# Two kv heads in one 4 MB unit: larger transfers and fewer slots in a decode attention kernel

## The chip, the cores and the metric

The kernel runs on one core of one Trainium2 chip. The core has a matrix engine (PE, whose weight loads the profile lists apart as PEld), a vector engine (DVE), a scalar engine (ACT), a general engine (POOL) and a queue engine (SP). In this kernel SP issues every transfer between HBM and the on-chip memory (SBUF, 128 partitions); sixteen DMA engines carry them out. Matrix products land in PSUM, eight banks of 512 fp32 numbers for each partition.

The metric is device time in microseconds for one launch. Before the change it is 667.16 us, the median of three runs (666.79 to 667.6). The profiled execution that all rows below come from has a span of 665.6 us, measured from its first instruction to its last.

## What is computed

One decoding step for four sequences (B = 4, one token each, D = 512) through attention, a gated feed-forward block (FFN), and the same two again with the same caches and weights:

```python
        rep = Hq // Hkv
        q = (lambda x, *d: x.transpose(*d))((x @ wq).reshape(B, Sq, Hq, Dh), 0, 2, 1, 3)
        k = jnp.repeat(k_cache, rep, axis=1)
        v = jnp.repeat(v_cache, rep, axis=1)
        scores = jnp.einsum("bhqd,bhkd->bhqk", q, k) * (Dh ** -0.5)
        p = _softmax(scores, axis=-1)
        o = jnp.einsum("bhqk,bhkd->bhqd", p, v)
        return (lambda x, *d: x.transpose(*d))(o, 0, 2, 1, 3).reshape(B, Sq, Hq * Dh) @ wo
...
    def _B_ref(x, w_gate, w_up, w_down):
        g = _silu(x @ w_gate)
        u = x @ w_up
        return (g * u) @ w_down
...
    x = A_x
    x = x + _A_ref(_layernorm(x, axis=-1), A_k_cache, A_v_cache, A_wq, A_wo)
    x = x + _B_ref(_layernorm(x, axis=-1), B_w_gate, B_w_up, B_w_down)
    x = x + _A_ref(_layernorm(x, axis=-1), A_k_cache, A_v_cache, A_wq, A_wo)
    x = x + _B_ref(_layernorm(x, axis=-1), B_w_gate, B_w_up, B_w_down)
    return x
```

All inputs are bf16; Hq = 32, Hkv = 8, Sk = 8192, Dh = 128, F = 1792, so four query heads share a kv head. The two caches hold 4 x 8 x 8192 x 128 numbers each, 67 MB. Each layer reads both. What SBUF can keep from the first layer for the second spares 12 MB of the second reading.

## The kernel before

A unit is one kv head of one sequence: its 8192 keys are 2 MB, its values another 2 MB. There are 32 units for each layer (`NU`). A unit lies in SBUF as 128 partitions of 64 tokens, 16 KB for each partition, so one transfer is 128 rows of 16 KB. SBUF holds eight such slots (`NSLOT`, L139). Six (`NKEEP`) end the first layer with keys and values of the last three units, and the second layer begins with these; the other two take the FFN weights `wg`, `wd` and a part of `wu` at the end of each layer. The other three quarters of `wu` stay in SBUF once loaded.

For each unit, in eight blocks q of eight tokens for each partition:

- `turn` (L393): DVE transposes a block of keys in place, in 32x32 squares of fp32 words (128x512).
- `scores` (L413): four matmuls, each with a 128x128 stationary made of the query (`zq`, written by POOL in `place_q`, L404) and 256 moving key columns. All eight blocks add up in one PSUM bank, whose 128 rows are block, square and query head.
- The softmax of the unit, in steps that `line` spreads over the following blocks: `max_p` on DVE (L419), `max_t` on PE and DVE (L423, L426), `exps` on PE and ACT (L435 to L441), `turn_p` (L444), which transposes the probabilities into `pT`, and `total` (L447, L449) for the sums.
- `values` (L494): 64 matmuls, each with 128x128 values as the stationary and 32 moving columns of `pT`; then `scale_o` (L502).

After four units of a head, `out_proj` (L521) multiplies with `wo` and adds to `x`. `center`, `deviation`, `qproj` and `ffn` do the rest between the layers. `qproj` ends with products on 32-row strips of the output (L573) that place the query for the scores.

The order on PE is written by the program: `blocks` holds what PE is to do next, with a cost for each, and `drain` lets PE lag about 2 us behind the transposes that DVE was given; `advance` lets the steps in `line` in after so much PE work. The keys of a unit come first, then the values of the unit before. All engines run their instructions in order. SP too issues in the order of `items`: `pump` stops at the first one that finds no free slot. At the end of a layer, loads are kept out of slots 6 and 7 (`late`), so that the FFN weights follow the last values directly. The last values of each layer come in four parts (`split`); after the first layer's gate product the place of the weights, and later that of the first kept keys, is refilled in parts (`load_part`).

Resources are tracked by name in `_Sync`: an instruction waits for what last wrote what it reads, and for what last read or wrote what it writes. The first transfer, `A_x` into `scr` (L626), waits for nothing.

Of the kernel before, what the change touches and what calls it, by code (L numbers as in the profile page):

```python
# [5 lines left out]
ACTF = mybir.ActivationFunctionType  # L6
# [97 lines left out]
def bass_interleave_layers__gqa_block_cached__swiglu_ffn__decode_kernel(  # L104
# [17 lines left out]
    REP = Hq // G  # L122
    P = 128
    assert Dh == P and B * Hq == P and D % P == 0 and F % P == 0 and B == 4
# [3 lines left out]
    TT = S // P  # L128
    TB = 8
    NB = TT // TB  # L130
    QB = 32
    NA = P // QB
    assert NB * REP == QB and 2 * 2 * QB == Dh
    SW = TB * QB
    XQ = B * Hq
    assert XQ <= SW
    ZP = QB - REP
    NQ = 4
    NSLOT = 8  # L139
    NKEEP = 6  # L140
    WIDE = 32
    NU = B * G
# [3 lines left out]
    with ExitStack() as es:  # L146
        sb = lambda name, shape, dt: es.enter_context(nc.sbuf_tensor(name, shape, dt))


        SL = TT * Dh  # L150
        FR = KT - 1
        kvf = sb("kvf", [P, NSLOT * SL + FR * F], BF16)
        kv = kvf[:, 0:NSLOT * SL].rearrange("p (s w) -> p s w", s=NSLOT)
        f0 = NKEEP * SL
        wg_sb = kvf[:, f0:f0 + KT * F].rearrange("p (k f) -> p k f", k=KT)
        wu_sb = [kvf[:, NSLOT * SL + k * F:NSLOT * SL + (k + 1) * F] for k in range(FR)]
        wu_sb.append(kvf[:, f0 + KT * F:f0 + (KT + 1) * F])
        f1 = f0 + (KT + 1) * F
        assert f1 + FO * D <= NSLOT * SL
        wd_sb = kvf[:, f1:f1 + FO * D].rearrange("p (f n) -> p f n", f=FO)  # L160
        places = [f"s{s}.{q}" for s in range(NKEEP, NSLOT) for q in range(NB)]
        room = lambda a, b: places[(a - f0) // (TB * Dh):(b - 1 - f0) // (TB * Dh) + 1]
        at_w = {"wg": room(f0, f0 + KT * F) + ["wg"], "wu": room(f0 + KT * F, f1) + ["wu", "wu3"],
                "wd": room(f1, f1 + FO * D)}
        WD = ((0, 6), (6, 12), (12, 14))
        wq_sb = sb("wq_sb", [P, KT, HqDh], BF16)
        wo_sb = sb("wo_sb", [P, Hq, D], BF16)
        identf = sb("identf", [P, P], FP32)

        ident = identf[:].bitcast(BF16).rearrange("p (x e) -> p x e", e=2)[:, :, 1]  # L170
        onesf = sb("onesf", [P, 1], FP32)
        quad = sb("quad", [P, NA], BF16)
        head = sb("head", [P, REP], FP32)
        xT = sb("xT", [P, XB], FP32)
        xs = sb("xs", [P, B], FP32)
        vs = sb("vs", [P, B], FP32)
        xx = sb("xx", [P, XB], FP32)
        lnv = sb("lnv", [P, B], FP32)
        rstd = sb("rstd", [P, B], FP32)
        eps_sb = sb("eps_sb", [P, 1], FP32)  # L180
        lsc_sb = sb("lsc_sb", [P, 1], FP32)
        zero_sb = sb("zero_sb", [P, 1], FP32)
        xc = sb("xc", [P, XB], FP32)
        xn = sb("xn", [P, XB], BF16)
        oT = sb("oT", [P, Hq, B], BF16)
# [507 lines left out]
```

## Time and profile before

| | us |
|---|---|
| median of 3 runs | 667.16 (666.79 to 667.6) |
| span of the profiled execution | 665.6 |
| PE busy, matmuls | 495.1 |
| DVE busy | 380.8 |
| ACT busy | 89.9 |
| DVE transposes of keys, L393, 488 of them | 313.1 |
| PE scores, L413, 2048 of them | 330.0 |
| PE values, L494, 4096 of them | 123.9 |
| DVE idle ahead of L393, waiting for keys | 197.1 |

Transfers move 273.89 MB; the mean over the span is 413 GB/s. A row of the group lists reads: line, engine, operation, output <- inputs, shapes, count, then busy time in us, the mean duration of one in ns, and the idle time of the engine just before them with what ended it. Matmuls overlap in the PE pipeline, so the busy time of one is longer than the distance from one start to the next; the distance is what a row of matmuls costs.

### The profile page before, as it was taken

How to read it: one execution, taken by the hardware profiler on the slowest of the kernel's cores; microseconds unless marked ns; L12 is line 12 of the kernel's file. 1: busy time of each engine (PE TensorE's matmuls, PEld its weight loads, DVE VectorE, ACT ScalarE, POOL GpSimd, SP SyncE). 2: the span in 40 equal slices, each digit the busy share in tenths (PEclk: the TensorE clock that was granted, in tenths of full speed). 3: DMA queues.
4: the chain of work that ended last, by engine and by line, in shares of the span. 5: the costliest groups of instructions: out<-in, count | busy, mean ns of one | idle time of the engine just before them, and what ended most of it. 6: DMA issues, size and time to landing. Idle time of an engine off the chain costs nothing.

```text
span 665.6 us, 16777 instructions
## 1 busy us (share of the span) xinstructions
PE 495.1 (74%) x7400; PEld 393.8 (59%) x7400; DVE 380.8 (57%) x879; ACT 89.9 (14%) x331; POOL 19.9 (3%) x75
## 2 busy tenths in 40 slices
PE   1766676876877777777875999886777787687786
PEld 1554555654755555556665878764665565465565
DVE  1645465664765665665641279775566565476572
ACT  1010111111101101101110112110111111110120
POOL 0000000000000000000000000000000000000000
PEclk9987787777788777878685979977878777778895
DMA  8999999999999999999999999999999999999995
GB/s 357 417 412 405 419 427 426 424 426 427 427 427 422 428 429 425 426 424 427 426 404 367 332 408 425 432 423 424 428 427 426 426 425 426 427 428 425 423 417 226
DMA packets 27320, 274.96 MB, mean 413 GB/s; under 512 B 2408, under 2 KB 6512, under 8 KB 11120
## 3 DMA queue, kind: packets, MB, share of 16 engines
q1 hardware_dynamic: 27248, 273.89, 98.4%
q8 instruction: 58, 0.95, 0.6%
q14 instruction: 14, 0.11, 0.0%
HBM read 273.88 MB, written 0.00 MB: 411 GB/s over the span
## 4 chain that ended last, share of the span: by engine, by line
DMA 68%; PE 16%; SPq 10%; DVE 3%; issue 2%; POOL 0%; ACT 0%; DVEq 0%; POOLq 0%
DMA kvf<-in_A_k_cache_dram 63%; PE ps L413 10%; SPq L93 10%; DMA kvf<-in_B_w_down_dram 5%; PE ps L494 3%; DVE kvf L393 2%; PE ps L435 1%; PE ps L423 1%; DVE pT L444 0%; PE ps L559 0%; DVE mx L419 0%; PE ps L447 0%; PE ps L610 0%; DVE rl L449 0%; PE ps L573 0%
## 5 line engine op out<-in xcount | busy, mean ns | idle before, releaser
L393 DVE STREAM_TRANSPOSE kvf<-kvf 128x512 f32<-128x512 f32 x488 | 313.1, 677 | 197.1 <-DMA kvf<-in_A_k_cache_dram 197.1
L413 PE MATMUL ps<-kvf,zq 128*128 128x256 bf16 x2048 | 330.0, 317 | 9.5 <-DVE kvf L393 5.9
L413 PEld LDWEIGHTS ps<-kvf,zq 128*128 128x128 bf16 x2048 | 212.5, 112 | 71.0 <-DVE kvf L393 11.3
L494 PE MATMUL ps<-pT,kvf 128*128 128x32 bf16 x4096 | 123.9, 179 | 34.9 <-DVE rl L449 32.6
L494 PEld LDWEIGHTS ps<-pT,kvf 128*128 128x128 bf16 x4096 | 120.5, 97 | 42.8 <-issue 37.4
L423 PE MATMUL ps<-identf,mx 128*1 128x128 f32 x64 | 19.8, 309 | 95.7 <-DVE mx L419 95.7
L429 ACT ACTIVATE pb<-m 1x128 f32<-1x128 f32 x64 | 19.7, 308 | 401.6 <-DVE m L426 401.6
L423 PEld LDWEIGHTS ps<-identf,mx 128*1 128x1 f32 x64 | 5.2, 81 | 99.9 <-DVE mx L419 99.8
L404 POOL TENSOR_TENSOR zq<-scr,quad 128x64 bf16<-128x64 bf16 x64 | 18.8, 294 | 617.2 <-PE ps L413 549.2
L435 PEld LDWEIGHTS ps<-onesf,pb 1*128 1x128 f32 x128 | 24.1, 234 | 20.5 <-issue 17.4
L444 DVE STREAM_TRANSPOSE pT<-pb 128x256 bf16<-128x256 bf16 x64 | 26.9, 420 | 13.4 <-ACT pb L439 13.1
L419 DVE TENSOR_REDUCE mx<-ps 128x1 f32<-128x256 f32 x64 | 25.1, 393 | 9.8 <-PE ps L413 9.8
L439 ACT ACTIVATE pb<-ps,nm 128x256 bf16<-128x256 f32 x64 | 30.4, 475 | 2.1
L435 PE MATMUL ps<-onesf,pb 1*128 1x1 f32 x128 | 29.6, 298 | 0.6 <-ACT pb L429 0.5
L438 ACT ACTIVATE nm<-ps 128x1 f32<-128x1 f32 x64 | 11.0, 171 | 132.7 <-PE ps L435 132.7
L447 PEld LDWEIGHTS ps<-rsm,onesf 128*128 128x128 f32 x128 | 20.4, 200 | 2.6 <-ACT rsm L441 0.6
L447 PE MATMUL ps<-rsm,onesf 128*128 128x4 f32 x128 | 19.7, 224 | 0.5 <-ACT rsm L441 0.5
L426 DVE TENSOR_REDUCE m<-ps 1x4 f32<-1x128 f32 x64 | 15.9, 249 | 7.0 <-PE ps L423 6.6
L441 ACT ACTIVATE rsm<-head,rs 128x4 f32<-128x4 f32 x64 | 19.0, 297 | 2.1
L502 DVE TENSOR_TENSOR oT<-ps,rl 128x4 bf16<-128x4 f32 x64 | 7.9, 123 | 10.4 <-PE ps L494 10.1
L559 PE MATMUL ps<-xn,wq_sb 128*128 128x4 bf16 x256 | 7.7, 165 | 8.2 <-DMA wq_sb<-in_A_wq_dram 8.2
L521 PEld LDWEIGHTS ps<-oT,wo_sb 128*128 128x128 bf16 x256 | 8.9, 105 | 6.4 <-DVE oT L502 3.9
(55 smaller groups left out, 91.4 us busy)
## 6 DMA issues: line engine op xcount, KB each, us to landing
kvf<-in_A_k_cache_dram SPq DMA_DIRECT2D x59, 2048.0 KB, 31.3
kvf<-in_A_v_cache_dram SPq DMA_DIRECT2D x58, 2048.0 KB, 32.3
wq_sb<-in_A_wq_dram SPq DMA_DIRECT2D x4, 1024.0 KB, 8.1
wo_sb<-in_A_wo_dram SPq DMA_DIRECT2D x4, 1024.0 KB, 19.2
kvf<-in_A_v_cache_dram SPq DMA_DIRECT2D x8, 512.0 KB, 18.7
kvf<-in_B_w_gate_dram SPq DMA_DIRECT2D x2, 1792.0 KB, 23.3
kvf<-in_B_w_down_dram SPq DMA_DIRECT2D x4, 768.0 KB, 16.4
kvf<-in_A_v_cache_dram SPq DMA_DIRECT2D x2, 1024.0 KB, 6.8
```

Source lines behind the costliest of these rows:

```text
L93: ins = self.eng[engname].dma_start(out_ap, in_ap)
L393: T.op("dve", lambda e: e.transpose(w, w), reads=[f"s{s}.{q}"], writes=[f"s{s}.{q}"])
L413: T.op("pe", lambda e: e.matmul(bank(bk)[:, 0:SW], lhsT=zq[:, c, z0:z0 + P], rhs=w[:, :, c // 2, :, c % 2], start=(q == 0 and c == 0), sto ...
L419: T.op("dve", lambda e: e.tensor_reduce(mx[:], bank(bk)[:, 0:SW], AX.X, ALU.max), reads=[f"pb{bk}"], writes=["mx"])
L423: T.op("pe", lambda e: e.matmul(bank(STEP)[0:1, 0:P], lhsT=mx[:], rhs=identf[:], is_transpose=True, start=True, stop=True), reads=["mx", " ...
L429: T.op("act", lambda e: e.activation(mrow.rearrange("p (x h) -> p x h", h=REP), m4[:].unsqueeze(1).to_broadcast([1, QB, REP]), ACTF.Copy), ...
L435: T.op("pe", lambda e: e.matmul(bank(STEP)[:, 0:1], lhsT=mrow, rhs=onesf[0:1, :], start=True, stop=True), reads=["pb", "onesf"], writes=[f ...
L439: T.op("act", lambda e: e.activation(pb[:], bank(bk)[:, 0:SW], ACTF.Exp, bias=nm[:], accum_out=rs[:]), reads=[f"pb{bk}", "nm"], writes=["p ...
L441: T.op("act", lambda e: e.activation(rsm[:], head[:], ACTF.Copy, scale=rs[:]), reads=["head", "rs"], writes=["rsm"])
L444: T.op("dve", lambda e: e.transpose(pT[:, turn_of[u], 0:SW], pb[:]), reads=["pb"], writes=[f"pT{turn_of[u]}"])
L447: T.op("pe", lambda e: e.matmul(bank(TOT)[:, 0:REP], lhsT=ones, rhs=rsm[:], start=True, stop=True), reads=["rsm", "onesf"], writes=[f"pb{T ...
L494: T.op("pe", lambda e: e.matmul(bank(bk)[:, 0:WIDE], lhsT=kv[:, s, t * Dh:(t + 1) * Dh], rhs=pT[:, turn_of[u], c0:c0 + WIDE], start=(t == ...
```

## The change

A unit becomes a pair of neighbouring kv heads of one sequence. Its keys are 4 MB, as 128 rows of 32 KB (64 partitions for each head), and so are its values; there are 16 pairs (`NP`) for each layer and four slots of 32 KB. Three slots end the first layer with the keys of the last pair and the values of the last two. The order of all loads, with slots and parts, is now a list written ahead (`cmds`); `freed` returns single blocks of a slot, and `pump` issues the next entry when all its blocks are free.

- `turn` takes 128x1024 words, eight of them for a pair (248 in all, from 488). `scores` takes 512 columns instead of 256 (1024 matmuls, from 2048).
- `values` is turned round: the stationary is 32 columns of probabilities, of which `turn_p` fills the half that belongs to the partition's head, the rest being zero, and 512 columns of values stream past it. The outputs of four successive matmuls go to four 32-row strips of one bank. 32 matmuls for a pair, 1024 in all, from 4096. `gather` (four DVE operations on 128x128 words) and `combine` (one matmul and one DVE operation) then pick out and add up what belongs together; nothing of that was there before.
- `exps` loses two ACT operations; the broadcast of the maximum is one small matmul and one DVE operation that multiplies and sums (L464 after). `total` now stands ahead of `turn_p`. `pT`, `rl` and `oT` lose their second copies or shrink. `exps` of a pair now follows the values of the pair before (`behind`), since there is one `pT`.
- In the first layer `qproj` handles all 32 heads at once, ahead of the first keys; in the second eight, then 24 (4 and 28 before). It copies its result by four DVE operations where one did it.
- The FFN weights share one slot with keys and values: slot 0 in the first layer, slot 1 in the second. Slightly less of `wu` stays in SBUF (64 KB more to load in the second layer).
- Small tiles move into `pb`: `A_x` is now loaded into `pb` too, where DVE at the start writes and reads intermediate tables.

The core of the diff:

```diff
-    TB = 8
-    NB = TT // TB
...
+    NP = G // 2 * B
+    TT = 2 * S // P
+    NB = 8
+    TB = TT // NB
...
-    NSLOT = 8
-    NKEEP = 6
...
+    NSLOT = 4
...
+        T.op("dve", lambda e: e.tensor_reduce(pbf[:, 0:QB],
+                                              identf[:].rearrange("p (j x) -> p x j", j=NA), AX.X, ALU.max),
+             reads=["ident"], writes=["pb"])
+        T.op("dve", lambda e: e.tensor_reduce(sel[:].rearrange("p (h r) -> p h r", h=2),
+                                              pbf[:, 0:QB].rearrange("p (h q r) -> p h r q", h=2, q=QH), AX.X, ALU.max),
+             reads=["pb"], writes=["sel"])
+        T.op("dve", lambda e: e.tensor_reduce(own[:], pbf[:, 0:QB].rearrange("p (h q r) -> p q h r", h=2, q=QH),
+                                              AX.XY, ALU.max),
+             reads=["pb"], writes=["own"])
...
+        order = [list(range(NP)), [NP - 1, NP - 2] + list(range(NP - 2))]
...
+        cmds += [(("W", 0), W_SLOT[0], 0, NB)]
+
+        us = order[1]
+        cmds += [(K(1, us[1]), 0, 0, 3), (K(1, us[1]), 0, 3, 4), (K(1, us[1]), 0, 4, NB)]
+        cmds += [(K(1, us[2]), 1, q, q + 2) for q in range(0, NB, 2)]
+        rest = []
+        for i in range(3, NP):
+            rest += [K(1, us[i]), V(1, us[i - 1])]
+        rest.append(V(1, us[-1]))
+        ring = (0, 3, 1, 2)
+        for i, it in enumerate(rest):
+            s = ring[i % NSLOT]
+            if i == 0:
+                cmds += [(it, s, q, q + 2) for q in range(0, NB, 2)]
+            elif i == 1 or i == len(rest) - 1:
+                cmds += [(it, s, q, q + NB // 2) for q in range(0, NB, NB // 2)]
+            else:
+                cmds.append((it, s, 0, NB))
+        cmds += [(("W", 1), W_SLOT[1], 0, NB)]
...
+                    need = {(s, q) for q in range(a, b)}
+                    if not need <= free:
+                        return
+                    free.difference_update(need)
+                    if it[0] == "W":
+                        load_weight("W", it[1], s)
+                    else:
+                        slot_of[it] = s
+                        load(it, a, b, sem_s[s] if b - a == NB else part_sem())
...
+        def freed(s, a, b):
+            free.update((s, q) for q in range(a, b))
+            pump()
...
-            T.op("dve", lambda e: e.transpose(pT[:, turn_of[u], 0:SW], pb[:]), reads=["pb"], writes=[f"pT{turn_of[u]}"])
+            for h in range(2):
+                hp = slice(h * (P // 2), (h + 1) * (P // 2))
+                dst = pT[hp].rearrange("p t n (h x) -> p t n h x", h=2)[:, :, :, h, :]
+                T.op("dve", lambda e: e.transpose(dst, pb[hp]), reads=["pb"], writes=["pT"])
...
+                    step = lambda gap, fn: [gap, u, lambda: fn(u)]
+                    line.extend([step(0.0, max_p), step(1.2, max_t)])
+                    behind.extend([step(0.9, exps), step(1.0, total), step(0.3, turn_p)])
+                    if alone:
+                        line.extend(behind)
+                        behind.clear()
...
-                    T.op("pe", lambda e: e.matmul(bank(bk)[:, 0:WIDE], lhsT=kv[:, s, t * Dh:(t + 1) * Dh],
-                                                  rhs=pT[:, turn_of[u], c0:c0 + WIDE], start=(t == 0), stop=(t == TT - 1)),
-                         reads=[f"s{s}.{q}", f"pT{turn_of[u]}"], writes=[f"pb{bk}"], sig=(t % TB == TB - 1))
...
+                for t in range(t0, t0 + TB // 2):
+                    j = t % NA
+                    first, stop = (h == 0 and t < NA), (h == NH - 1 and t >= TB - NA)
+                    T.op("pe", lambda e: e.matmul(bank(OBK)[j * QB:(j + 1) * QB, :], lhsT=pT[:, t, h, :], rhs=v[:, :, t, :],
+                                                  start=first, stop=stop),
+                         reads=[f"s{s}.{q}" for q in range(h * QH, (h + 1) * QH)] + ["pT"], writes=[f"pb{OBK}"],
+                         sig=(t % (TB // 2) == TB // 2 - 1))
+                if i % 2:
+                    finished(V(L, u), h * QH, (h + 1) * QH)
+                if i == 3:
+                    done.add((L, u))
+                    line[0:0] = rest_
+                    line.extend(behind)
+                    behind.clear()
...
+            def gather():
+                o = lambda q: bank(OBK)[:, q * Dh:(q + 1) * Dh]
+                T.op("dve", lambda e: e.tensor_scalar(acc, o(0), own[:, 0:1], None, op0=ALU.mult),
+                     reads=[f"pb{OBK}", "own"], writes=PB)
+                for q in range(1, QH):
+                    T.op("dve", lambda e: e.scalar_tensor_tensor(acc, o(q), own[:, q:q + 1], acc, op0=ALU.mult, op1=ALU.add),
+                         reads=[f"pb{OBK}", "own", "pb"], writes=["pb"])
+
+            def combine():
+                T.op("pe", lambda e: e.matmul(bank(CMB)[:, 0:H2], lhsT=acc, rhs=sel[:], start=True, stop=True),
+                     reads=["pb", "sel"], writes=[f"pb{CMB}"])
+                T.op("dve", lambda e: e.tensor_tensor(oT[:, gp % 2, :, b], bank(CMB)[:, 0:H2], rl[:], ALU.mult),
+                     reads=[f"pb{CMB}", "rl"], writes=[f"oT{gp % 2}"])
+
+            rest_ = [[0.0, None, gather], [1.3, None, combine]]
+            blocks.extend((0.9, lambda i=i: part(i)) for i in range(4))
...
-        T.dma("sp", xio, A_x.rearrange("b s d -> (b s) d"), sem_x, writes=SCR)
+        T.dma("sp", xio, A_x.rearrange("b s d -> (b s) d"), sem_x, writes=PB)
```

## The prediction

> **What bounds the kernel now.** I read the forty slices first, then the chain of waits, then windows, and then the timeline at the start, between the layers and at the end.
>
> ```profile
> DMA  8999999999999999999999999999999999999995
> GB/s 357 417 412 405 419 427 426 424 426 427 427 427 422 428 429 425 426 424 427 426 404 367 332 408 425 432 423 424 428 427 426 426 425 426 427 428 425 423 417 226
> ...
> q8 instruction: 58, 0.95, 0.6%
> ...
> DMA 68%; PE 16%; SPq 10%; DVE 3%; issue 2%; POOL 0%; ACT 0%; DVEq 0%; POOLq 0%
> ```
>
> The DMA engines are full nearly throughout, at 426 GB/s; 68% of the chain is DMA. A slice is 16.64 us. Against 426 the slices lose about 5 us at the start, 7 to 8 in slices 20 to 23 (the FFN between the layers) and 8 at the end. So what counts is the rate in the steady part, and how long the queue is dry at three places.
>
> ```profile
> 336.00:340.00 4.00, 4.00 (x89) 3.72 (x90) 2.56 (x7) 1.03 (x4) 0.00 (x0) 1.00 0.99 402
> 345.00:349.00 4.00, 1.43 (x28) 1.15 (x24) 1.12 (x7) 0.00 (x0) 0.00 (x0) 0.50 1.04 405
> 100.00:320.00 220.00, 165.44 (x2317) 129.05 (x2314) 132.79 (x295) 28.85 (x108) 6.46 (x22) 0.81 1.01 426
> ```
>
> Windows: the last three columns are granted clock, DMA share and GB/s. Rows of 3.5 and 4 KB move at 402 to 405, rows of 16 KB at 426.
>
> **The change, part by part.**
>
> *Steady part, on the path.* One packet on one of 16 engines takes 142 ns for 3584 bytes (405/16 = 25.3 GB/s) and 615 ns for 16384 (426/16). The line through both has 9 ns for each packet. Rows of 32 KB save half of the packets: 9/1231 = 0.7% of the 600 us that 255.9 MB of keys and values take, 4.4 us. No row of 32 KB is in the trace, so the ends are -4.4 and, if such rows are cut in two, 0; a loss (+3, half a per cent) I can't exclude. I take -3, nearer to the line. Instructions are fetched by the same engines (q8, 0.95 MB); matmuls go from 7264 to 3088, so some 0.5 MB less, -1.3 at 426 GB/s. Sum -4.3, ends -5.7 and +1.7.
>
> *Engines in the steady part, hidden behind DMA.* A pair of units arrives every 19.7 us (8.4 MB at 426).
>
> ```profile
> 28.01 0.40 PE L573 MATMUL ps<-pT,identf 128*32 128x112 bf16 x16 [0.37 <-DVE pT L564]
> ...
> 363.57 5.80 PE L413 MATMUL ps<-kvf,zq 128*128 128x256 bf16 x32 [0.78 <-POOL zq L404]
> ...
> 372.16 1.50 PE L413 MATMUL ps<-kvf,zq 128*128 128x256 bf16 x12
> ...
> 634.60 2.46 DVE L393 STREAM_TRANSPOSE kvf<-kvf 128x512 f32<-128x512 f32 x4
> ```
>
> Scores: 12 in 1.50 us, less the 0.27 that the last takes, is 0.11 us each at full clock; half that speed at half clock. 512 columns take 0.22 or 0.43, so a block of four 0.9 or 1.7, a pair 7 or 13.7 (7 or 13.7 for two units before). Values: the row L573 shows 16 matmuls of 112 columns on four 32-row strips, 0.40 us less a duration of 0.21, 12.7 ns each, where 112 columns alone need 48. Four strips run at once. So 32 matmuls of 512 columns are 8 rounds, 1.7 or 3.4 us (before 2 x 64 x 28 ns = 3.6, hidden too). DVE for a pair: eight transposes of 1024 at 1.2 (two of 0.615), 9.6; maximum over 512, 0.66 (256 took 0.39); minimum row 0.25; `gather`, four at 0.31 (between 56 and 256 words from PSUM, 0.22 and 0.39), 1.25; L464 0.35; `turn_p` 1.4 (256 columns took 0.42, so 0.84 to 1.7 for two of 512); rest 0.3. Sum 13.8 of 19.7, with waits for PE 15. A slot is free about 15 us before its next load is due (keys scored at 14.4, the load that takes their place begins at 29.5). So the new DVE work, ACT's loss of two operations and POOL's 32 instead of 64 `place_q` lie behind DMA; what it costs without that cover is rival 3. The 64 KB more of `wu` are 0.15 us, in the rounding.
>
> *Start.* `A_x` is the first in SP's queue, and `wq` and all caches stand behind it.
>
> ```profile
> 0.75 0.36 SPq L93 DMA_DIRECT2D scr<-in_A_x_dram  x1
> ...
> 1.27 0.09 DVE L247 MEMSET pT<- 128x32 uint32 x1
> ...
> 1.51 0.38 DVE L248 TENSOR_REDUCE head<-identf 128x4 f32<-128x128 f32 x1 [0.15 <-POOL quad L239]
> ...
> 2.17 0.18 PEld L632 LDWEIGHTS ps<-identf,scr 4*128 4x128 bf16 x4 [2.17 <-DMA scr<-in_A_x_dram]
> ```
>
> Now it goes to `pb`, and so waits for the three new reductions there. On DVE: `pT`'s memset starts at 1.27 and takes 0.5 for 512 words (312 took 0.32), `head` 0.4, the next 0.4, `sel` and `own` 0.2 each, with gaps 3.1. SP issues at 3.15 instead of 0.75: +2.4 for everything behind in SP's queue, and DMA has no slack to take it back (ends 2.0 and 2.8).
>
> *End.* In the list of loads the last values go to slot 1 and so do the weights of the second layer, which wait until PE has used all of these values. Nothing but the output stands behind them in SP's queue, but the whole last FFN waits for them. Before, the weights (4.13 MB) followed the values without a gap.
>
> ```profile
> kvf<-in_A_v_cache_dram SPq DMA_DIRECT2D x1, 512.0 KB, 21.3
> ...
> 661.63 1.01 PE L610 MATMUL ps<-scr,kvf 128*128 128x4 bf16 x32 [0.60 <-DMA kvf<-in_B_w_down_dram]
> ```
>
> The last part of the values, issued at 630.4, lands 21.3 later, at 651.7; PE is done with it at 653.1; the wait for `wd` ends at 661.63, 9.9 after the values. In the changed kernel, from the landing of the last keys (t = 0) the values land at 2 x 9.8 = 19.7. DVE in its order: transpose, maximum of the pair before, its minimum, a transpose, `gather`, six transposes with L464 and a reciprocal between, `turn_p`: 14.9 with the waits. Maximum of the last pair to 15.7; its transposed row and minimum 16.4; second half of the values before, 17.2; `gather` 18.5; `combine` 0.6 (0.59 for L534, also fp32) 19.1; L461 and L464, 19.9; exponentials of 512, 1.0 with the sum, and `rsm` 0.3, 21.2; total and reciprocal 0.8, 22.0; `turn_p` 23.4; values, PE being cold, 3.4 + 0.2, 27.0. That is 7.3 after the landing. Issue to data takes 1.5 (`A_x`: 0.75 to 2.17), and the weights 10.5 at 400 GB/s: 19.4 after the landing instead of 9.9. +9.5. Ends: +6.5 (`turn_p` 0.84, warm PE) and +11.5.
>
> *Between the layers.* Before: the values land at 344.6 (T), the FFN ends at T + 14.3, held by `wd`, the scores of the kept keys start at 363.57 (T + 19), and two more slots' worth, 8 MB, is in at 382.9 (last part issued 374.3, 8.6 to landing): T + 38.3. After: values done at T + 7.3, `gather`, `combine`, 32 matmuls of `out_proj`, centre: the gate starts at T + 12.2, ends at 14.3 (2.1, as before) and frees the first blocks; the queue has been dry for 1.8 us. FFN ends at 18.2. Then 4.65 as before plus 1.0 for twice the heads and three more copies: scores at 23.9. Their first two blocks, cold, 3.4: load at 27.4, data at 28.9, where the 4 MB before ended at 25.6; dry for 3.3. The 8 MB are in at T + 38.7, +0.4. But the next full load, keys into slot 1, waits until the third pair there is scored: DVE goes without a pause from T + 34 through the second kept pair (7.2 for six blocks, 1.4 for its maxima and sums, 1.4 for `turn_p`), the third's first block and `gather` (1.2 + 0.9 + 1.25), waits for the second `qproj` (96 matmuls at 28 ns, 1.0 of copies) to 51.6 and has the third pair's other seven blocks by 61.7, scored 62.5, data 64. The two loads between end at 38.7 + 19.7 = 58.4: dry for 5.6, with the next values behind it in SP's queue. Together +6.0; ends +1 and +10.
>
> [...]
>
> Sum: -4.3 + 2.4 + 9.5 + 6.0 = +13.6 on 665.6, 679.2. The median of the runs was 1.56 above this span: **680.8 us**.
>
> **Rivals.**
>
> 1. *Rows of 32 KB run much faster* (not slower than before). The 61 loads of 4 MB that it needs take 9.85 each at 426. To give back the other 17.9 us (2.4 + 9.5 + 6.0) less 1.3 of fetches, each must save 0.27: 438 GB/s decides. At 445, 26 us are saved, and 658 is left. For it: two windows early in the trace read 433 to 436 (7 to 13 and 13 to 26 us). Against it: with no time for packets at all the line gives 433. [...]
> 2. *Values are not run four at once.* 32 x 0.43 = 13.7 instead of 3.4: +10 at the end, +10 and two times 5 between the layers: 711. L573 speaks against it.
> 3. *The pair's work on DVE and PE exceeds 19.7 us*, and the steady part follows it: at 22 us, 29 pairs x 2.3 = 67, 748. It needs 5 us above my 15.
> 4. *The rows are cut in two by the hardware*: it doesn't do what it says. 683.8, within my range.
>
> **How the numbers follow.** Forecast 0.65, rival 4 0.12, rival 2 0.05, rival 3 0.04, rival 1 0.11, something that ends within 0.2% 0.03. The lower ends together (-5.7 + 2.0 + 6.5 + 1) give 671, the upper (1.7 + 2.8 + 11.5 + 10) 693; I stop at 690, since all four at once are unlikely. So the range is 671 to 690. Rivals 2, 3, 1 and the last case, 0.23 together, lie mostly outside it. A difference under 0.2% (1.3 us) can't be told from none here: faster 0.11, same 0.03, slower 0.86.
>
> **What would show it.** The steady windows at 426 to 430 GB/s and fewer packets than before; DVE waiting for keys once in 19.6 us; L573's successor and the values with starts in groups of four; SP's first issue near 3.1; a hole in GB/s after the last values, of about 9 us, with the weights' issue behind PE's last values; after the FFN two or three holes, the last near 60 us after the values' landing. Wrong I am if the steady rate is off 424 to 431, or if the slots are free so early that the holes close.

## The result and the profile after

The changed kernel takes 677.66 us by the median of four runs (676.26 to 679.29), the kernel before beside it 666.97: a ratio of 1.0159, 95% interval 1.0138 to 1.018. It is slower by 1.6%. The sum of the prediction was +13.6 us on the span; the profiled execution spans 677.2 instead of 665.6, +11.6 (675.3 and +9.7 in a second profile, below). One run of the kernel before and one of a later experiment (all5) took 886 and 883 us where all others of the same kernel lie within 1%; these two are slow executions and are left out everywhere below.

The page of the kernel after, from the forty slices (16.93 us each), the DMA queues and the chain:

```profile
DMA  7999999999999999999978989999999999999946
GB/s 310 433 430 406 431 423 412 431 434 433 428 433 428 429 434 427 434 431 429 420 267 317 394 346 422 431 434 433 430 427 431 432 429 432 431 432 431 422 189 250
DMA packets 19090, 274.44 MB, mean 405 GB/s; under 512 B 1512, under 2 KB 5872, under 8 KB 9456
...
q8 instruction: 25, 0.41, 0.2%
...
DMA 59%; DVE 18%; PE 17%; issue 2%; another core or an unknown queue 2%; SPq 1%; ACT 0%; POOL 0%; ACTq 0%; DVEq 0%
```

The steady slices, counted from 0, are higher than before (427 to 434 in slices 8 to 18, where there was 422 to 429), and the three places where the queue runs dry are deeper: the first slice, the slices 20 to 23 between the layers (267, 317, 394, 346) and the last two. DVE, 3% of the chain before, now holds 18%.

The trace's completions of the transfers give the sum stage by stage. A transfer counts as landed when the last of its 16 DMA engines has landed; "units" are the 4 MB units of keys and values, counted in the order in which they arrive.

```
                                   before   after    change   prediction
first issue (A_x)                    0.75     2.61    +1.9     +2.4
32 units in (layer 0), landed      344.60   341.58
  so the steady part of layer 0                       -4.9   \
38 units in, landed                422.56   428.89             > steady, both layers: -4.3
  so between the layers, 32 to 38   77.96    87.31    +9.4   | between: +6.0
61 units in (all), landed          651.72   652.48           /
  so the steady part of layer 1    229.16   223.59    -5.6
from there to the end               13.88    24.72   +10.8     +9.5
span                               665.6    677.2    +11.6    +13.6
```

Start and end came nearly as worked out. The steady part gained 10.5, more than twice the 4.3 of the sum and outside its bounds, and the stage between the layers lost 3.4 more than its term (1.4 in the second profile).

The start and the end in the timeline of the kernel after (start, duration, engine, line, operation; in brackets the idle time before and what ended it):

```profile
2.41 0.18 DVE L283 TENSOR_REDUCE tiny<-pb 128x4 f32<-128x32 f32 x1
2.61 0.36 SPq L93 DMA_DIRECT2D pb<-in_A_x_dram  x1
...
647.64 0.69 DVE L447 TENSOR_REDUCE tiny<-ps 128x1 f32<-128x512 f32 x1 [0.21 <-PE ps L441]
...
655.63 3.60 PE L527 MATMUL ps<-kvf,pT 128*32 128x512 bf16 x32 [1.70 <-DVE pT L474]
...
659.31 0.38 SPq L93 DMA_DIRECT2D kvf<-in_B_w_gate_dram  x1
...
673.19 1.01 PE L663 MATMUL ps<-pb,kvf 128*128 128x4 bf16 x32 [1.08 <-DMA kvf<-in_B_w_down_dram]
```

SP issues `A_x` as soon as the third reduction on `pb` is done. At the end the last keys landed at 633.0; their maximum is taken at 647.6, the last values (landed 652.5) are multiplied from 655.6 to 659.2, and only then, at 659.31, are the weights of the second layer issued. The last wait for `w_down` ends at 673.19, 20.7 after the values' landing; before the change it was 9.9. The working had 27.0 from the keys' landing to PE's last values and 19.4 from the values' landing to the end of that wait; it became 26.2 and 20.7.

Between the layers (timeline, then windows of 4 us; the last three columns of a window are granted clock, DMA share and GB/s):

```profile
344.25 3.49 PE L527 MATMUL ps<-kvf,pT 128*32 128x512 bf16 x32 [1.70 <-DVE pT L474]
...
349.18 0.82 SPq L93 DMA_DIRECT2D kvf<-in_B_w_up_dram  x2
...
361.10 1.03 PE L663 MATMUL ps<-pb,kvf 128*128 128x4 bf16 x32 [2.24 <-DMA kvf<-in_B_w_down_dram]
...
376.53 0.69 DVE L447 TENSOR_REDUCE tiny<-ps 128x1 f32<-128x512 f32 x1 [7.26 <-PE ps L441]
```

```profile
344.00:348.00 4.00, 3.49 (x32) 1.24 (x32) 0.31 (x2) 0.00 (x0) 0.00 (x0) 0.56 0.62 246
348.00:352.00 4.00, 1.81 (x36) 1.66 (x36) 1.72 (x7) 0.00 (x0) 0.00 (x0) 0.86 0.42 127
...
368.00:372.00 4.00, 4.00 (x13) 1.38 (x11) 1.28 (x2) 0.00 (x0) 0.00 (x0) 0.58 0.34 135
...
400.00:404.00 4.00, 2.62 (x13) 0.96 (x11) 3.93 (x5) 0.00 (x0) 0.00 (x0) 1.00 0.75 315
404.00:408.00 4.00, 3.91 (x42) 1.28 (x41) 3.50 (x5) 0.00 (x0) 0.30 (x1) 1.00 0.48 135
```

Three holes are to be seen, at 344 to 352, 368 to 372 and 400 to 408. The second and the third are those of the working (loads that wait for the kept heads' scores, and the full load that waits for slot 1). The first is new: the second piece of `w_up`'s third row block is issued at 349.18, although its slot had been free since 326. It bears the name and the semaphore of the first piece, which lands at 349.16; SP waits for that, and behind it in SP's queue stand the rest of `w_up` and all of `w_down`. So the FFN's last wait ends only at 361.1.

### The profile page after: what moved, and what is told of

It reads as the page before. It is cut to its first block, busy times and chain, and to the rows that moved or that the text cites. A ratio compares the mean times of both kernels' runs of the same rounds, so it can differ in the third digit from the quotient of the medians.

```text
span 677.2 us, 7647 instructions
## 1 busy us (share of the span) xinstructions
PE 431.4 (64%) x3192; PEld 179.3 (26%) x3192; DVE 420.9 (62%) x705; ACT 38.5 (6%) x107; POOL 10.7 (2%) x43
## 2 busy tenths in 40 slices
DMA packets 19090, 274.44 MB, mean 405 GB/s; under 512 B 1512, under 2 KB 5872, under 8 KB 9456
## 4 chain that ended last, share of the span: by engine, by line
DMA 59%; DVE 18%; PE 17%; issue 2%; another core or an unknown queue 2%; SPq 1%; ACT 0%; POOL 0%; ACTq 0%; DVEq 0%
DMA kvf<-in_A_k_cache_dram 52%; DVE kvf L421 12%; PE ps L441 9%; PE ps L527 5%; DMA kvf<-in_B_w_up_dram 3%; DMA kvf<-in_B_w_down_dram 3%; DVE pT L474 2%; DVE pb L546 1%; DVE tiny L447 1%; SPq L93 1%; PE ps L451 1%; PE ps L567 1%; PE ps L605 0%; DVE pb L543 0%
## 5 line engine op out<-in xcount | busy, mean ns | idle before, releaser
L421 DVE STREAM_TRANSPOSE kvf<-kvf 128x1024 f32<-128x1024 f32 x248 | 295.9, 1219 | 159.8 <-DMA kvf<-in_A_k_cache_dram 159.7
L441 PE MATMUL ps<-kvf,zq 128*128 128x512 bf16 x1024 | 285.9, 420 | 19.5 <-DVE kvf L421 13.0
L441 PEld LDWEIGHTS ps<-kvf,zq 128*128 128x128 bf16 x1024 | 95.8, 108 | 173.9 <-issue 59.5
L451 PE MATMUL ps<-identf,tiny 128*1 128x128 f32 x32 | 11.2, 350 | 172.1 <-DVE tiny L447 172.1
L527 PE MATMUL ps<-kvf,pT 128*32 128x512 bf16 x1024 | 91.2, 492 | 11.8 <-DVE pT L474 11.8
L466 ACT ACTIVATE pb<-ps,tiny 128x512 bf16<-128x512 f32 x32 | 22.0, 687 | 587.2 <-DVE tiny L464 395.0
L474 DVE STREAM_TRANSPOSE pT<-pb 64x512 bf16<-64x512 bf16 x64 | 43.7, 682 | 1.1
L527 PEld LDWEIGHTS ps<-kvf,pT 128*32 128x32 bf16 x1024 | 26.6, 111 | 55.5 <-issue 47.0
L546 DVE SCALAR_TENSOR_TENSOR pb<-ps,tiny,pb 128x128 f32<-128x128 f32 x96 | 33.7, 351 | 3.4
L447 DVE TENSOR_REDUCE tiny<-ps 128x1 f32<-128x512 f32 x32 | 21.2, 661 | 7.5 <-PE ps L441 7.5
L550 PEld LDWEIGHTS ps<-sel,pb 128*128 128x128 f32 x64 | 13.6, 223 | 16.4 <-DVE pb L546 10.3
L477 PE MATMUL ps<-rsm,tiny 128*128 128x8 f32 x64 | 11.8, 256 | 6.2 <-ACT rsm L468 6.0
L477 PEld LDWEIGHTS ps<-rsm,tiny 128*128 128x128 f32 x64 | 10.2, 190 | 18.4 <-ACT rsm L468 17.5
L461 PEld LDWEIGHTS ps<-m,tiny 1*128 1x128 f32 x64 | 9.5, 185 | 13.6 <-issue 12.4
L461 PE MATMUL ps<-m,tiny 1*128 1x8 f32 x64 | 12.4, 264 | 0.2 <-DVE m L454 0.2
## 6 DMA issues: line engine op xcount, KB each, us to landing
kvf<-in_B_w_gate_dram SPq DMA_DIRECT2D x2, 1792.0 KB, 13.6
```

The source lines that it names most:

```text
L421: T.op("dve", lambda e: e.transpose(w, w), reads=[f"s{s}.{q}"], writes=[f"s{s}.{q}"])
L441: T.op("pe", lambda e: e.matmul(bank(bk)[:, 0:SW], lhsT=zq[:, z0:z0 + P], rhs=w[:, :, c // 2, :, c % 2], start=(q == 0 and c == 0), stop=( ...
L447: T.op("dve", lambda e: e.tensor_reduce(mx[:], bank(bk)[:, 0:SW], AX.X, ALU.max), reads=[f"pb{bk}"], writes=["mx"])
L451: T.op("pe", lambda e: e.matmul(bank(STEP)[0:1, 0:P], lhsT=mx, rhs=identf[:], is_transpose=True, start=True, stop=True), reads=["mx", "ide ...
L461: T.op("pe", lambda e: e.matmul(bank(STEP)[:, 0:H2], lhsT=onesf[0:1, :].to_broadcast([1, P]), rhs=m8[:], start=True, stop=True), reads=["m ...
L466: T.op("act", lambda e: e.activation(pb[:], bank(bk)[:, 0:SW], ACTF.Exp, bias=nm, accum_out=rs), reads=[f"pb{bk}", "nm"], writes=PB + ["rs"])
```

## The experiments

All start from the changed kernel and differ from it only in the edit shown. The base is that kernel again, run beside the first group.

> The changed kernel once more, as the base of the runs beside it. Its four times so far lie in two groups, 676.3 and 679.1, so a step has to be worth more than about 2 us to be seen in the times alone; smaller ones are read from the trace. Expected: 677.7, within 1.5.

Measured: 677.27 (676.78 to 678.92). All eight times of this kernel have the median 677.3, and two groups can be seen. The two profiles (spans 677.2 and 675.3) differ by more than 0.4 first where the parts of `w_down` land in layer 0, the last at 361.71 and 359.48. From there one is some 2 later to the end; why was not followed. Below, gains in time are against 677.3, and stages against this second profile, in which 32 to 38 units take 85.4 and the end 24.65. In the five profiles whose edits leave the stage between the layers as it is (this kernel twice, x_own, w_slot2, end_both) 32 to 38 units take 84.9 to 87.3, so a difference of 1 or 2 in that stage alone says little.

**The start.**

```
-  e.tensor_reduce(pbf[:, 0:QB], identf...)            writes=["pb"]
+  mask = scr[:].bitcast(FP32)[:, 0:QB]
+  e.tensor_reduce(mask, identf...)                    writes=["qr0"]
```

> The reductions at the start write into scr instead of pb, so that A_x waits for nothing. My theory (the start term): SP's first issue goes from 2.61 back to about 0.75, every load behind it comes 1.9 earlier, and since no engine sets the pace in layer 0, the last values of layer 0 land at 339.7 instead of 341.6 and the end comes 1.9 earlier, 675.8. Rival: the stages behind are not moved by the loads alone (the hole at 400 to 408 us is ended by DVE), then the 1.9 is lost there and the time stays 677.7.

Measured: 674.77 (674.75 to 674.98), 2.5 less. `A_x` is issued at 0.75, layer 0's last values land at 339.50 instead of 341.28, and the span is 2.5 shorter. My theory holds; nothing behind swallowed it.

**The end, by parts.**

```
-  W_SLOT = (0, 1)
+  W_SLOT = (0, 2)
```

> The second layer's weights go to slot 2, freed by the values before the last, instead of slot 1. Both theories: the weights are issued long before, follow the last values without a gap, and the last of them lands 10 to 11 us after the values, near 663. Theory A, that of the prediction (the wait for the slot is the whole loss at the end, +10.8): the last wait for wd ends near 662.5 and the span falls by about 10.8, to 666.4. Theory B (the longer chain of the last pair takes over): the last values are used up only 6.8 after they landed, at 659.3, the gate starts at 664 instead of 666.4, TensorE needs 3.3 for gate and up, the activation ends 2.6 later, down takes 2, the rest 3: the end is at 673.1, a gain of 4.1.

Measured: 673.51 (673.07 to 673.64), 3.8 less; from the values' landing to the end 20.1 instead of 24.65. Theory B. The timeline of this kernel:

```profile
654.09 3.61 PE L527 MATMUL ps<-kvf,pT 128*32 128x512 bf16 x32 [1.70 <-DVE pT L474]
...
662.61 0.89 PE L644 MATMUL ps<-xn,kvf 128*128 128x4 bf16 x28 [0.36 <-DVE pb L586]
...
666.59 1.65 PE L663 MATMUL ps<-pb,kvf 128*128 128x4 bf16 x56 [0.43 <-DVE pb L658]
```

No matmul of the FFN waits for a DMA any more (the weights are in at 661.54); each waits for DVE. What holds the end is that the last values, landed at 651.1, are only used from 654.1 to 657.7.

```
-  if i == 0:
+  if i in (0, len(rest) - 3):           # layer 1; in layer 0 likewise
       cmds += [(it, s, q, q + 2) for q in range(0, NB, 2)]
```

> The last keys of each layer are loaded in four parts of 1 MB instead of one of 4 MB, so that their transposes begin 7.3 earlier. My theory: the last values are then used up about 1.5 to 2 after they landed, not 6.8. At the end that is 5 us (the weights still wait for the slot), between the layers nothing by itself, since there the weights' last part ends the FFN's wait: 672.7. Rival 1: DVE has no room for the earlier transposes (the pair before is still on it), gain under 1. Rival 2: the 5 come back at both places: 667.7.

Measured: 672.67 (671.46 to 673.65), 4.6 less. The weights are issued at 652.51, 2.2 after the last values landed (650.27); in the base it is 6.8. The end takes 20.2, and 32 to 38 units take 84.2, only 1.2 less. My theory: the late use of the values is worth about 4.5 at the end and little between the layers.

> w_slot2 and the second layer's half of k15_parts together; all else as in the changed kernel (base 677.3 by the median, span 675.3). Theory A (the two causes of the loss at the end are the slot and the late scores, and together they are all of it): the last values are used up 2 us after they landed, the last weights land 10.5 to 11 after the values, and from the values' landing to the end it takes 13.9 as before the change instead of 24.7: span 664.6, time 666.5. Theory B (they only add as measured alone, -4.1 and -4.9 in span): 666.3, time 668.3. Theory C (they overlap, the longer of the two stays): 670.5, time 672.5.

Measured over ten runs: 669.15 (667.59 to 671.31), 8.1 less; the end takes 16.2. The two add nearly (4.5 each alone, 8.5 together): theory B. Against the 13.9 before the change 2.3 stay. The timeline shows what holds them:

```profile
650.25 3.60 PE L527 MATMUL ps<-kvf,pT 128*32 128x512 bf16 x32 [1.70 <-DVE pT L474]
...
662.50 0.54 PE L663 MATMUL ps<-pb,kvf 128*128 128x4 bf16 x14 [0.43 <-DVE pb L658]
663.67 1.26 PE L663 MATMUL ps<-pb,kvf 128*128 128x4 bf16 x42 [0.63 <-issue]
```

The values of the last pair take 3.6 (in the kernel after they take the same 3.60, there at a granted clock of 0.50 from 655.6 to 659.3), and the chain from there to the FFN runs without a wait for DMA: PE reaches `w_down` at 662.5, 10.8 after the values' landing, where before the change the transfer itself ended the wait at 9.9.

**Between the layers.**

```
-  A B_w_up piece FY: of row block FR -> sem_w["wu"][1], writes=["wu1"]
+                                     -> sem_w["wu"][3], writes=["wu3"]
```

> The four parts of w_up get a semaphore and a name each; in the changed kernel two of them share one, so that SP waits until the first has landed (349.2) before it issues the rest of the weights, and the queue runs dry from 346 to 351. My theory: the queue goes on without a pause there, the last of the weights lands near 355.5 instead of 361.7, w_down ends at 358.7 instead of 362.1, and with it all of the second layer's work comes 3.4 earlier: 674.3. Rival 1: the loads after it wait for slots that the kept keys free, at their old time, and the hole only moves to 362 to 372 or to 400 to 408: gain under 1. Rival 2: the whole 5.4 that the keys of the third pair were late against the prediction comes back: 672.3.

Measured: 674.95 (674.75 to 675.22), 2.3 less; 32 to 38 units take 82.5, 2.9 less. The windows:

```profile
344.00:348.00 4.00, 3.44 (x32) 1.24 (x32) 0.41 (x1) 0.00 (x0) 0.00 (x0) 0.50 1.03 395
348.00:352.00 4.00, 1.75 (x38) 1.44 (x34) 1.78 (x7) 0.00 (x0) 0.00 (x0) 0.50 1.01 373
352.00:356.00 4.00, 3.45 (x94) 3.39 (x95) 1.38 (x9) 0.81 (x3) 0.00 (x0) 0.50 0.24 89
```

The hole at 344 to 352 is filled, and a shorter one opens at 352 to 356, where the next keys wait for the FFN to free their blocks. The last weights land at 355.43 instead of 359.48, PE no longer waits for them, and `w_down` ends at 358.8 instead of 359.9. The load into slot 1 that ends the third hole is issued 59.6 after the values' landing instead of 62.2. Between my theory (3.4, counted from the slower of the two profiles) and rival 1: the wait was real and is worth 2.3 in time, clear of the base, since all four times (674.75 to 675.22) lie below all eight of it (676.26 to 679.29). Of the 4.1 by which the weights come earlier, the end of the FFN gains 1.1, because the work of DVE and PE now ends it.

```
-  drain(LAG)
+  if L == 0 or u != order[1][1] or q == NB - 1:
+      drain(LAG)
```

> In the second layer all eight blocks of the second kept pair are transposed before the maximum of the first, which stands ahead of six of them in DVE's order and waits for TensorE from 369.3 to 376.5. My theory: DVE's backlog after the FFN is 7.3 shorter, of which some 5 can be used (the last blocks land at 371.8); the keys of the third pair are scored near 400 instead of 405.5, slot 1 is free 5 earlier, and the dry stretch from 403 to 407 goes almost away: end 4 earlier, 673.7. Rival 1: the maximum, now later on DVE, delays that pair's values and the queue runs dry somewhere else: gain under 1. Rival 2: the second qproj, behind which TensorE is idle, holds the third pair: gain 2.

Measured: 676.24 (674.19 to 676.56), 1.0 less, which the spread of the base hardly tells from nothing, in the time as in the stage; the load into slot 1 that ends the third hole is issued at 401.35 instead of 403.51, and 32 to 38 units take 84.4, 1.0 less. At most rival 1's gain, and not shown to be more than none. DVE's own timeline:

```profile
377.64 0.28 DVE L454 TENSOR_REDUCE m<-ps 1x8 f32<-1x128 f32 x1 [1.90 <-PE ps L451]
...
388.07 0.26 DVE L611 TENSOR_TENSOR scr<-ps,tiny 128x96 bf16<-128x96 f32 x1 [0.96 <-PE ps L606]
...
389.75 2.36 DVE L421 STREAM_TRANSPOSE kvf<-kvf 128x1024 f32<-128x1024 f32 x2
```

The idle 7 us went, but DVE now waits in short pieces for PE's answers, and most of the third pair's transposes still stand behind the second `qproj` at 388.

**The steady part.** Two parts of the change save DMA time there, longer rows and fewer instructions to fetch. The first run undoes the rows alone:

```
+  if b - a == NB:                        # a full load: two of 2 MB
+      T.dma("sp", kv[:, s, 0:SL // 2], src[:, 0:SL // 2], sm)
+      a = NB // 2
   T.dma("sp", kv[:, s, a * BW:b * BW], src[:, a * BW:b * BW], sm, writes=names)
```

> Each load of 4 MB is issued as two of 2 MB with 16 KB rows; waits, slots and all other work stay. Theory A (9 ns for a packet): 16 packets more on each engine for each pair of units, 0.144 us, 30 pairs: 4.3 in all; the first of the 16 engines to land layer 0's last values is later by 2.1, the distance between the first and the last engine stays 3.7. End at 682. Rival 1 (the rows are worth nothing, the steady gain came from fewer instruction fetches): 677.7. Rival 2 (the whole steady gain of 10.5, measured by the slowest engine, is from the rows): 688.

Measured: 680.44 (677.73 to 682.45), 3.2 more, with a wide spread: between theory A and rival 1. In the trace the steady part of both layers loses 3.7 by the last engine, and the table below decides for theory A. The second undoes most of the saving in instructions and keeps the rows:

```
-  matmul(bank(OBK)[32 rows, :],             lhsT=pT[:, t, h, :], rhs=v[:, :, t, :])
+  for q in range(QH):
+      matmul(bank(OBK)[32 rows, q * Dh:...], lhsT=pT[:, t, h, :], rhs=v[:, q, t, :])
```

> Each value matmul of 512 columns becomes four of 128, on the same four strips: 3072 matmuls more, some 0.4 MB of instructions, so the instruction queue goes from 25 packets back to about 49 (58 before the change); rows stay 32 KB. Theory A (a fetch of 16 KB holds one engine up for about 1.1 us, and the slowest engine gets more than its share): the first engine to land stays, the distance to the last at the end of layer 0 grows from 3.7 to about 6, and the steady part loses 4 in all: 681 to 682. Rival (a fetch costs its bytes only): 0.4 MB at 426 GB/s, 0.9 us: 678.6. TensorE has 36% to spare, so it should not set the pace in either.

Measured: 683.32 (681.03 to 683.73), 6.0 more. The profiled execution is the fastest of the four, and its span is 3.9 above the base's: by the last engine the steady part loses 1.5 in layer 0 and 2.6 in layer 1, theory A's 4, the stage between the layers loses 1.2 and the end gains 1.3. By the first engine the steady part loses nothing. The 2.3 from this execution to the median are not explained by any trace. The third adds instructions on an engine that issues neither transfers nor matmuls in this kernel:

```
   place_q(u)
+  for k in range(176):                      # in 27 of the 32 pairs
+      T.op("pool", lambda e: e.memset(idle[:, k % 44:k % 44 + 1], 0), ...)
```

> As the changed kernel, with 176 memsets of one byte on GpSimd, which is idle, after each of 28 of the 32 place_q: 4928 instructions more, about 0.32 MB or 19 packets on the instruction queue, with no matmul more and the same rows. This parts the fetch from the matmuls that values128 added. Theory A (the packets that fetch instructions hold up single DMA engines): the first engine's pace stays at 19.43 for a pair of units, the distance from the first engine to the last at the end of layer 0 grows from 3.2 to 3.7 to about 4.8, in layer 1 from 2.3 to about 4.3; the last values land 3 later and the time is 680 to 681. Rival (it was the matmuls or TensorE's reading of SBUF that slowed some engines in values128): distances 3.2 to 3.7 and 2.3 as in the changed kernel, time 677.3.

Measured: 697.03 (696.29 to 697.47), 19.8 more: theory A by its mechanism and far off in size (the last values land 20 later and not 3). (The edit skips five pairs, not four: 4752 memsets.) The completions of the 16 engines tell the three apart. The pace is the time for a pair of units, 8 MB, over nine pairs of layer 0:

```
             pace of the    mean of      pace of the    first to last engine
             first engine   the 16       last engine    when layer 0 is in
before          19.58         19.75         19.90             6.5
after           19.44         19.50         19.57             3.7
base again      19.44         19.50         19.58             3.2
rows16          19.58         19.65         19.73             3.3
values128       19.42         19.57         19.76             5.0
pool_idle       19.46         19.56         20.30            12.4
```

Halving the rows costs every engine 0.14 to 0.15 a pair, 9 ns for each of the 16 additional packets, and leaves the distances. More instructions leave the first engine as it was and delay the last. No run undoes both; if the two add, 0.15 and 0.18 bring the 19.58 of the base to 19.91, where the kernel before has 19.90. The queues, first of values128, then of pool_idle (its q8 has 25 packets, as in the changed kernel):

```profile
q8 instruction: 49, 0.80, 0.5%
```

```profile
q14 instruction: 46, 0.38, 0.1%
```

GpSimd's instructions came over another queue, q14, in packets of 8 KB: 46 instead of 9. The mean pace rose by only 0.06 (by the bytes it would be 0.03: 0.31 MB over 27 pairs at 430 GB/s), while the last engine's rose by 0.72. The landings show that this is one engine: at the end of layer 0 fifteen engines are in within 1.8 of the first, and one comes 12.4 after it; at the end of layer 1 it is 2.5 and 11.2. That engine loses some 19 us, which is 0.5 for each of the 37 packets more if all of them fall on it. The trace does not name the engine. It does show that GpSimd itself holds up nothing: it is busy 25% of the span, and PE waits for its `place_q` as long as before (3.5 us in all). What the memsets' writes to SBUF do to DMA was not tested without their fetches.

One place shows a single packet at work. In the first profile of the changed kernel the last `w_up` part of layer 1 lands on all 16 engines within 0.46, up to 667.69; at 667.62 q8 begins to fetch 16 KB, which takes 1.09. The next part, the first of `w_down`, lands on fifteen engines within 0.45 and on one 1.53 later, and the two parts behind it keep that distance. The eight other profiles whose weights are issued only after the last values show the same, 1.1 to 1.7, each with one q8 packet at that time. That the late engine is the packet's is read from the time alone. PE waits for that engine: it goes on at 673.19, when the second part of `w_down` is in on it (673.14), and the other fifteen were in by 671.70.

**All together.** The five edits x_own, w_slot2, wu_own, turns_first and k15_parts:

> All five edits: x_own, w_slot2, wu_own, turns_first and k15_parts in both layers. If the losses lie at three separate places they add: span 675.3 less 1.9 at the start, less 10.8 at the end, less 2.3 (weights without a pause) and 1.7 (values used up earlier, until the weights' landing holds the FFN) and 1 to 2 (transposes first) between the layers: 656.6 to 657.6, time 658.5 to 659.5, faster than the kernel before by 1.2%. Rival: the dry stretch near 400 us keeps its end (it hangs on the second qproj and on the third pair's transposes behind it), and what is gained between the layers is 2 at most: 660.6 to 662.

Measured: 660.91, the median of four runs (660.52 to 661.85), a ratio of 0.990 to the kernel before, 95% interval 0.9886 to 0.9914: faster than both. The page:

```profile
GB/s 364 430 413 416 439 412 413 436 431 430 431 430 429 432 435 426 435 427 418 430 407 363 379 397 420 424 439 422 439 427 431 436 420 439 427 433 426 431 409 188
```

Stage by stage against the kernel before: start 0, steady -4.8 and -4.0, 32 to 38 units 78.0 (before 78.0), the end 17.0 (before 13.9), in sum -5.6. So between the layers everything has come back: 7.4 against the base, where wu_own, turns_first and k15_parts alone gave 2.9, 1.0 and 1.2. That each alone had left the next wait in place would explain it; no run was made to show it. The 2 us that are missing from what I expected are at the end and not, as the rival has it, near 400: I had put in the whole 10.8, and end_both showed 8.5.

```
-  drain(LAG)
+  if L == 0 or u not in order[1][1:3] or q == NB - 1 and u == order[1][1]:
+      drain(LAG)
+  elif u == order[1][2]:
+      drain(5.0)
```

> As all5, and the third pair's transposes in the second layer may run five units of 0.9 us ahead of its scores instead of two, since in turns_first DVE was idle for some 8 us between 373 and 389 while those keys were landing. Theory: slot 1 is free 3 us earlier, the dry stretch before the fourth pair's keys shrinks by as much, 3 less than all5. Rival: the transposes wait for their parts and hold up the sums of the first two kept pairs that stand behind them on DVE, no gain or a loss of 1.

Measured: 662.59 (661.67 to 662.70), not better than all5; 32 to 38 units take 80.7 instead of 78.0. The rival: DVE now runs five of the third pair's transposes in a row, from 383.7 to 389.5, and what stands behind them, the sums of a pair (L467), comes at 389.4 instead of 385.7, its `turn_p` (L477) at 392.9 instead of 389.9, the load into slot 1 at 397.3 instead of 394.9.

## Why the prediction was right, and where it was not

*Direction and size.* The forecast of 680.8 was 3.1 too high, a rise of 2.0% for a measured 1.6%, and its range holds the result. It came out that well because the misses had opposite signs, 6 too little gained in the steady part against 3.4 and 1.3 too little lost between the layers and at the end. That is luck.

*Steady part: the mis-sized term.* The sum said "I take -3" for the rows, between -4.4 and 0, and "-1.3" for the fetches. The rows gave 0.14 x 30 = 4.2, the end that the line through two packets had shown; nothing in the trace spoke for less, and I drew back from it. The fetches were counted as bytes over 16 engines. But by the times a fetch falls on one engine (in pool_idle one engine came 12.4 after the first, with the last weights 1.53 after the other fifteen), and a load is ready when its slowest engine is (PE went on at 673.19, that engine was in at 673.14, the others by 671.70). By the first engine the steady pace gained 0.14 a pair, by the last 0.33, and rows16 and values128 part the two. By the last engine 10.5 was gained, so some 6 are left for the fetches; values128, which puts 24 of the 33 packets back, costs the steady part 4.1. The row stood on the page before: 58 packets hold 0.6% of 16 engines' span, 0.006 x 665.6 x 16 / 58 = 1.1 us each, where a data packet of the same size takes 0.62. Why a fetch takes longer than a data packet was not shown.

*Start.* +2.4 worked out, +1.9 measured, and x_own gave 2.5 back. The five operations on DVE take from 1.33 to 2.59, 1.3 in all, where the working has 1.8: `head` took 0.25 and not 0.4, and they follow one another without gaps.

*End.* +9.5 worked out, +10.8 measured. The chain itself was met within 1 us; the weights took 13.9 from issue to the last wait instead of 12.0, since the parts of `w_down` land 1.4 to 1.5 later on one engine than on the other fifteen, by all signs the one that had the instruction packet. What the working did not show is that the loss has two causes of about the same size, the slot that the weights wait for (w_slot2) and the late use of the last values (k15_parts).

*Between the layers: the step that failed.* The working let the FFN end 18.2 after the values, held by PE. It ended 20.6 after (361.1 + 1.0 against 341.58; 18.7 in the second profile), held by `w_down` in both. I had costed the additional `w_up` piece at "0.15 us, in the rounding" for its bytes and had not asked what its issue waits for, nor what stands behind it in SP's queue. wu_own showed 2.3 to 2.9 for it. The load into slot 1, worked out at 62.5 after the values, was issued 63.9 after them (62.2 in the second profile). That it fits is luck in part: wu_own, which like the working has no wait for the shared name, issues it at 59.6, so the working had some 3 too much on DVE's way there, and these stood in for the wait that it had left out. The rest of the miss, 2 us, lies behind that load: from its issue until 38 units are in it took 23.4 (23.2), where the working has 1.5 + 19.7.

*Engines hidden in the steady part.* Right: DVE waited 159.8 us for keys ahead of their transposes. The row of the page, by line, with the mean ns of one:

```profile
L421 DVE STREAM_TRANSPOSE kvf<-kvf 128x1024 f32<-128x1024 f32 x248 | 295.9, 1219 | 159.8 <-DMA kvf<-in_A_k_cache_dram 159.7
```

The 1.219 stands against 1.2, and the two halves of `turn_p` (L474), 0.682 each, against 0.7.

*The rivals.* Rival 1 (rows much faster) needed 438 GB/s; windows of 200 us hold 430 and 431. Rival 2 (values not four at once) falls by 16 matmuls of 512 columns in 1.05 us. Rival 3 (DVE and PE set the pace) falls by the 159.8 above. Rival 4 (rows cut in two) falls by the page's packets, 19,090, where rows16 has 27,011. And the sum has no term for strips that follow full matmuls; the timeline of the kernel after shows what that costs.

```profile
646.58 1.03 PE L441 MATMUL ps<-kvf,zq 128*128 128x512 bf16 x4
647.54 0.55 PEld L527 LDWEIGHTS ps<-kvf,pT 128*32 128x32 bf16 x16 [0.43 <-issue]
647.54 1.05 PE L527 MATMUL ps<-kvf,pT 128*32 128x512 bf16 x16
```

The first strip starts 0.31 after the last of the four full matmuls (647.54 against 647.23), where one full matmul follows another after 0.22; in all 30 places of this trace where strips follow full matmuls it is 0.31 or more. So such a place costs some 0.09, and ten of them, by my estimate five on each of the two chains (at the end and between the layers), under 1 us. The trace before held a like case, which the working overlooked: L435, on one row, starts 0.20 after a full matmul, where another full one starts 0.11 after (L447, fp32 like L435 but full, also 0.11). What the 0.09 is spent on was not shown. To have no term for it was right to within 1 us.

## What to carry to other kernels

A transfer was as late here as the latest of its engines (the steady part gained 0.14 a pair by the first engine and 0.33 by the last), so ask of each saving what it does to the slowest one and not to the mean. Every issue that a change adds has to be read with its waits and with all that is queued behind it; 64 KB cost over 2 us here because they shared a name and a semaphore (wu_own gave 2.3 back). With the larger units the steady part became cheaper (by 10.5 us) and the places where the stream breaks dearer (by 9.4 between the layers and 10.8 at the end), and it was the breaks (what the last unit waits for, what the first one waits for, which slot comes free last) that decided; once they were mended one by one, the larger units paid (660.91 us, 0.990 of the kernel before).

## What the runs showed of the hardware that was not expected

By the times, an instruction packet was paid here by one of the 16 DMA engines, and the loads waited for that engine: where one fetch of 16 KB on q8 fell among the last weights, one engine landed 1.1 to 1.7 us behind the other fifteen, in nine profiles. And 4752 memsets of one byte on an otherwise idle GpSimd, 0.31 MB of instructions more on q14, made the kernel 19.8 us slower: one engine came 12.4 us after the first at the end of layer 0, its pace up from 19.58 to 20.30 a pair, with the first engine's at 19.46 after 19.44. Rows of 32 KB instead of 16 KB saved 9 ns for each packet that fell away (19.44 instead of 19.58 a pair by the first engine, rows16), which over 30 pairs is 4 us and could be measured.
